# A windowed attention with a PReLU feed-forward in seven-product form: some sums kept in PSUM, bank copies that begin accumulations, 1024-column sums and splits, another ring and other combination buffers

## Chip, cores and metric

The kernel runs on one core of a Trainium2 chip. The metric is the device time of one execution in microseconds (us), lower is better; the time before is the median of three runs. Engines are named as in the profile: PE (TensorE, matmuls), PEld (its weight loads), DVE (VectorE), ACT (ScalarE), POOL (GpSimd), SP (SyncE, which here issues the DMAs). PSUM has eight banks of 512 fp32 columns by 128 partitions: PE writes its results there, and DVE and ACT read and write them.

## The reference

```python
# attention: batch 8, 8 heads, 576 positions, head size 64
scores = scale * np.matmul(q, k.transpose(0, 1, 3, 2))
mask_plain = (rel >= 0) & (rel < window)                                        # window 32, heads 0 to 3
mask_dil = (rel >= 0) & (rel < window * dilation) & (rel % dilation == 0)       # dilation 4, heads 4 to 7
scores = np.where(masks, scores, -1e9)
attn = softmax(scores)                                                          # sum + 1e-9 below
x = np.matmul(attn, v)                                                          # -> 4608 tokens x 512
# feed-forward
h = x @ w_in                                                                    # 512 x 2048
g = np.maximum(h, 0.0) + alpha * np.minimum(h, 0.0)
out = g @ w_out                                                                 # 2048 x 512
```

`w_in` and `w_out` come as 64-bit floats, all else as fp32.

## The kernel before, in words

Precision: every operand of the feed-forward is split in a high part (rounded to fp32r by an ACT copy) and a low part (the operand less its high part, a subtraction on DVE or POOL). A product is three matmuls (`PASSES`): high x high, high x low, low x high.

The tokens are nine tiles of `TT` = 512. Tiles 0 to 2 go the plain way, slice by slice of 128 hidden columns (`ffn_h`, L384, `ffn_y`, L431), while weights are loaded and converted and most pairs of heads go through attention (`Pair`). Its steps are scores (L200), maxima on DVE (L225), exponentials on ACT (L237), division on DVE (L244 to L247), transposes (L257), copies by ACT (L264), values (L275), and highs and lows or copies into the token tiles (L311 to L318). All engines' orders are written out by hand: what stands first in the code runs first on its engine.

**The combination stage.** From slice `SECOND - 1` on, POOL makes sums and differences of weight blocks for the later seven-product form (`combine`, L484 and L490, six instructions a block). Two slices later ACT rounds the result (`combined_high`, L494), DVE subtracts (`combined_low`, L498), and SP stores both parts (L502, L504). The results stand in two buffers, first in tag xB1, then in xA1. In a slice with scores, `combined_low` stands between the attention's scores and its maxima. The bank of the first scores is used next by a following `ffn_h`.

**The paired stage.** Tiles 3 to 8 go in three passes of two tiles, each pass in four groups, so twelve groups. A group takes two "units" of 256 hidden columns (j = 0, 1). Two token tiles by two halves of the model, and the same for the hidden columns, are multiplied as 2 x 2 block matrices with seven products instead of eight. A group has 28 steps of PE of six matmuls each: 14 for the hidden half (seven products q in `HORDER`, each for both j, `Four.mm`, L593) and 14 for the output half (seven products in `YORDER`, each for two column blocks m, `Out.mm`, L678). Every step takes one 256 KB weight block from a ring of `NRING` slots (`take`) and asks SP for the block that comes that many steps later (`feed`, L530).

Products of the hidden half accumulate in bank A (q 1, 6, 5, 3), B (q 2) and C (q 7, 4) of each unit. ACT saves bank A after q 1 (`s1`) and after q 6 (`s2`) and C after q 7 (`s7`), L620; DVE adds them back: 21 = C + s2, 22 = A + s7, 11 = B + s1 (L624), all into SBUF; 12 is A itself. The activation takes two instructions: `negative` on ACT (L634), `value` on DVE (L638). Then come the operands of the output half: T1 = 21 - 22, T2 = 11 - T1, T3 = 11 - 21, T4 = 12 - T2 on DVE (L645), and for each of the seven a high part on ACT (L648) and a low part (L652; "22" on DVE, the other six on POOL), all for each unit by itself, in 512 columns. The output products use 22, T1, T2, 11, T3, 12, T4 in the order of `YORDER`. After each product its bank is added to a running result in SBUF (L689; in the first group of a pass partly ACT copies, L687), 14 additions a group; in the last group of a pass the results are stored (L692).

`hidden` and `attention` put these operations at numbered steps. Attention for the last twelve pairs of heads lies in the first six groups, two pairs in each. In the last group of the first two passes the tiles of the next pass are split as well (`token_parts`, L573 to L578).

## Time and profile before

| | us |
|---|---|
| median of three runs | 1023.18 (1021.03 to 1023.5) |
| the profiled execution, own time | 1020.69 |
| its span, first to last instruction | 1018.9 |
| PE busy (share of the span) | 887.7 (87%) |
| DVE busy | 717.7 (70%) |
| ACT busy | 480.0 (47%) |
| POOL busy | 336.3 (33%) |
| mean granted clock of PE | 0.940 |

Busy time is summed per engine over the span, so it mixes stages with different limits. In a row of the timeline stand the start, the duration, engine, line, operation, output<-inputs and, in brackets, how long the engine had been idle and who released it. In a row of the lines view stand line, engine, operation, names, shapes and count, then busy us and mean ns of one, then idle time before. A row of the waits has who waited for whom, us in total, times, longest.

### The profile page before, as it was taken

The numbers are of one execution on the slowest core, as the hardware profiler recorded it, in microseconds if no ns is written. First come the engines' busy times: TensorE is split into PE (matmuls) and PEld (weight loads), VectorE is DVE, ScalarE is ACT, GpSimd is POOL, SyncE is SP. The second block draws the span as 40 slices with busy tenths as digits, with TensorE's granted clock in tenths as the row PEclk, the third lists the DMA queues.
The fourth block names the chain that finished last, engine by engine and source line by source line (L and its number), as shares of the span: only waits on it lengthen the run. The fifth ranks groups of instructions, "written<-read, shape, count | busy, mean of one in ns | idle before, by whom it ended". The sixth has DMA issues, their size and how long they took to land.

```text
span 1018.9 us, 21283 instructions
## 1 busy us (share of the span) xinstructions
PE 887.7 (87%) x7936; PEld 705.3 (69%) x7936; DVE 717.7 (70%) x1743; ACT 480.0 (47%) x1342; POOL 336.3 (33%) x250
## 2 busy tenths in 40 slices
PE   4679999898988989898989879898979797978887
PEld 4467888686877778676767657676758575766665
DVE  6997687877677666848666796848484877474756
ACT  6865555445354544554353554645242435333241
POOL 0000000407448930423324270606053527060615
PEclk9779999998999899999999989998989899989899
DMA  9730393169866664765656647664636484746452
GB/s 342 265 124 24 125 357 122 50 208 287 277 220 193 201 204 160 242 188 158 201 168 190 182 144 249 180 202 128 167 120 191 112 266 133 193 117 180 134 156 103
DMA packets 124229, 185.02 MB, mean 182 GB/s; under 512 B 9824, under 2 KB 61152, under 8 KB 124128
## 3 DMA queue, kind: packets, MB, share of 16 engines
q1 hardware_dynamic: 124128, 183.68, 58.5%
q8 instruction: 63, 1.03, 0.4%
q14 instruction: 38, 0.31, 0.1%
HBM read 143.79 MB, written 39.85 MB: 180 GB/s over the span
## 4 chain that ended last, share of the span: by engine, by line
PE 53%; DVE 27%; ACT 9%; issue 6%; POOL 3%; DMA 2%; SPq 0%; DVEq 0%; ACTq 0%; POOLq 0%
PE h L384 12%; PE y L431 10%; PE yA L678 8%; PE pA L593 7%; PE pC L593 5%; DVE stage L645 4%; DVE n L638 4%; DVE stage L638 4%; PE yB L678 3%; DVE stage L624 3%; PE yC L678 3%; ACT gp L648 2%; PE o L275 2%; ACT stage L634 2%; PE t L257 1%
## 5 line engine op out<-in xcount | busy, mean ns | idle before, releaser
L652 POOL TENSOR_TENSOR gp<-stage,gp 128x512 fp32r<-128x512 f32 x96 | 143.0, 1499 | 380.2 <-ACT gp L648 357.5
L384 PE MATMUL h<-x,w_dt.float32r 128*128 128x512 f32 x576 | 155.6, 424 | 19.6 <-DVE nm L225 19.2
L384 PEld LDWEIGHTS h<-x,w_dt.float32r 128*128 128x128 f32 x576 | 117.8, 208 | 46.7 <-issue 19.4
L431 PE MATMUL y<-g,w_dt.float32r 128*128 128x512 f32 x576 | 140.8, 393 | 0.0
L431 PEld LDWEIGHTS y<-g,w_dt.float32r 128*128 128x128 f32 x576 | 106.8, 188 | 22.7 <-ACT ob L443 0.4
L237 ACT ACTIVATE pr<-pr,nm 128x64 f32<-128x64 f32 (+1 forms) x240 | 80.5, 338 | 24.1 <-DVE nm L225 24.0
L645 DVE TENSOR_TENSOR stage<-n,stage 128x512 f32<-128x512 f32 x72 | 88.5, 1245 | 0.8
L484 POOL TENSOR_TENSOR wsum_xB<-w_dt.float32r 128x512 f32<-128x512 f32 x10 | 14.5, 1468 | 217.6 <-PE t L257 191.1
L648 ACT CAST gp<-stage 128x512 fp32r<-128x512 f32 x120 | 70.2, 613 | 26.1 <-DVE stage L645 25.8
L652 POOL TENSOR_TENSOR gp<-n,gp 128x512 fp32r<-128x512 f32 x48 | 78.1, 1626 | 0.0
L678 PE MATMUL yA<-gp,ring_w 128*128 128x512 f32 x192 | 57.4, 445 | 19.4 <-ACT gp L648 17.1
L678 PE MATMUL yA<-gp,ring_xA 128*128 128x512 f32 x192 | 56.5, 438 | 20.1 <-ACT gp L648 18.3
L411 ACT CAST g<-m 128x512 fp32r<-128x512 f32 x48 | 29.8, 621 | 80.2 <-DVE m L406 73.3
L689 DVE TENSOR_TENSOR py<-yA,py 128x512 f32<-128x512 f32 x78 | 53.0, 684 | 20.3 <-PE yA L678 20.1
L678 PE MATMUL yA<-gp,gp 128*128 128x512 f32 x144 | 46.3, 451 | 22.2 <-ACT gp L648 19.4
L624 DVE TENSOR_TENSOR stage<-pC,stage 128x512 f32<-128x512 f32 x24 | 16.5, 687 | 68.0 <-PE pC L593 64.1
L225 DVE CUSTOM_DVE_ANT_0 pr<-s,mask_sb 128x64 f32<-128x64 f32 (+1 forms) x288 | 45.1, 211 | 26.8 <-PE s L200 25.9
L678 PEld LDWEIGHTS yA<-gp,ring_w 128*128 128x128 f32 x192 | 39.5, 212 | 34.1 <-ACT gp L648 19.5
L620 ACT COPY stage<-pA 128x512 f32<-128x512 f32 x48 | 27.8, 583 | 74.8 <-PE pA L593 74.8
L678 PEld LDWEIGHTS yA<-gp,ring_xA 128*128 128x128 f32 x192 | 38.5, 207 | 34.7 <-ACT gp L648 21.3
L634 ACT ACTIVATE stage<-stage 128x512 f32<-128x512 f32 x48 | 30.1, 632 | 57.8 <-DVE stage L624 57.5
L678 PEld LDWEIGHTS yA<-gp,gp 128*128 128x128 f32 x144 | 29.4, 214 | 35.0 <-ACT gp L648 22.2
(135 smaller groups left out, 1874.0 us busy)
## 6 DMA issues: line engine op xcount, KB each, us to landing
ring_w<-wS SPq DMA_DIRECT2D x56, 256.0 KB, 2.9
ring_xA<-wS SPq DMA_DIRECT2D x56, 256.0 KB, 2.9
gp<-wS SPq DMA_DIRECT2D x56, 256.0 KB, 2.8
ring_w<-wO SPq DMA_DIRECT2D x56, 256.0 KB, 2.8
ring_xA<-wO SPq DMA_DIRECT2D x56, 256.0 KB, 2.9
gp<-wO SPq DMA_DIRECT2D x56, 256.0 KB, 3.0
v<-vW SPq DMA_DIRECT2D x24, 576.0 KB, 4.9
k<-kT SPq DMA_DIRECT2D x24, 288.0 KB, 4.4
```

What stands on the lines that cost most here:

```text
L237: nc.scalar.activation(out=self.pr[rows, r, :], in_=self.pr[rows, r, :], func=AF.Exp, bias=self.nm[rows, r:r + 1], scale=-1.0, accum_out=s ...
L384: nc.tensor.matmul(ms[t, f], lhsT=weight(0, a, f)[:, c * P:(c + 1) * P], rhs=half(t, c)[:, e, :], start=(c == 0 and n == 0), stop=(c == NC ...
L431: nc.tensor.matmul(ys[t][c], lhsT=weight(1, a, f)[:, c * P:(c + 1) * P], rhs=g[:, e, :], start=(first and n == 0), stop=(last and n == 2),)
L593: nc.tensor.matmul(to, lhsT=w[:, (2 * a + c) * P:(2 * a + c + 1) * P], rhs=part_of(name, e)[:, c * TT:(c + 1) * TT], start=start and c == ...
L624: nc.vector.tensor_tensor(out=self.x[n], in0=self.banks[bank], in1=self.x[term], op=ALU.add)
L634: nc.scalar.activation(out=self.m[n], in_=self.at(n), func=AF.Relu, scale=-1.0)
L638: nc.vector.scalar_tensor_tensor(out=self.m[n], in0=self.m[n], scalar=bal[:, f:f + 1], in1=self.at(n), op0=ALU.mult, op1=ALU.add)
L645: eng.tensor_tensor(out=self.x[n], in0=self.m[a], in1=self.x[b] if b[0] == "T" else self.m[b], op=ALU.subtract)
L648: nc.scalar.copy(out=self.g(n)[:, 0], in_=self.x[n] if n[0] == "T" else self.m[n])
L652: eng.tensor_tensor(out=g[:, 1], in0=self.x[n] if n[0] == "T" else self.m[n], in1=g[:, 0].bitcast(F32), op=ALU.subtract)
L678: nc.tensor.matmul(self.banks[what, m], lhsT=w[:, (2 * j + a) * P:(2 * j + a + 1) * P], rhs=g[:, e], start=start and j == 0 and n == 0, st ...
L689: nc.vector.tensor_tensor(out=to, in0=bank, in1=to, op=ALU.add)
```

## The change

- **Hidden half** (class `Hidden` for both units at once, in place of `Four`). Bank B is begun by an ACT copy of bank A after q 1 (`begin`), and q 2 accumulates on it, so 11 lies in B without an addition. 21 and 22 are added into PSUM (21 into its own bank C, 22 into a new bank D). `negative` and `value` read PSUM and write the wide SBUF tiles. T1, T2, T3 are one subtraction of 1024 columns for both units, and so are the high and low parts of 22, T1, 11, T2, T3, T4; T4's subtraction and the parts of 12 stay at 512. Low parts of 22, T1, T2, T3 are on DVE, those of 11, 12, T4 on POOL.
- **Output half.** Bank B is begun by an ACT copy of bank A after q 1, bank E after q 6; q 2 accumulates on B, q 3 on E, q 7 and q 4 on A. Five products are followed by an addition for each m (ten a group; plain DVE copies in the first group of a pass) into SBUF; 02, the sum of q 5, is added once to 22 and 12 at the end of a pass. `YORDER` changes from 1, 5, 6, 3, 7, 2, 4 to 1, 5, 6, 2, 7, 3, 4.
- **Attention in the groups** uses one pair of banks for scores, transposes and values, and the second pair of heads starts one step later. The split of the next tiles is placed a little later.
- **Ring**: ten slots in place of twelve; w2_1 holds the running 02 instead. Before the first group, four blocks are asked for at other slices, and six at the end.
- **Combination**: buffers also in xA0 and, later, a third one in w2_1; from the sixth block on, rounding comes three slices after POOL's work, not two. `combined_low` stands behind the maxima, the first exponentials, and the highs and lows of its slice.

```diff
-NRING = 12
+NRING = 10
...
     def combined(k):
-        tag = "xB1" if k < 5 else "xA1"
+        if k < 5:
+            tag, n = "xB1", k % 2
+        elif k < 9:
+            tag, n = ("xA1", "xA0")[(k - 5) // 2], (k - 5) % 2
+        else:
+            tag, n = (("xA1", 0), ("xA1", 1), ("w2_1", 0))[k % 3]
         if tag not in sums_at:
-            sums_at[tag] = const.tile([P, 2, 4, 2 * P], F32, tag=tag, name=f"wsum_{tag}")
-        return sums_at[tag][:, k % 2]
+            sums_at[tag] = const.tile([P, 1 if tag == "w2_1" else 2, 4, 2 * P], F32, tag=tag, name=f"wsum_{tag}")
+        return sums_at[tag][:, n]
...
-    YORDER = (1, 5, 6, 3, 7, 2, 4)
+    YORDER = (1, 5, 6, 2, 7, 3, 4)
...
-        if n >= 8:
-            return gblock(2, n // 2 - 4).rearrange("p e n -> p (e n)")[:, n % 2 * TT:(n % 2 + 1) * TT]
-        tag = ("w2_1", "w3_1", "xA1", "xA1")[n // 2]
+        if n >= 6:
+            return gblock("")[:, (n - 6) // 2, n % 2]
+        tag = ("w3_1", "xA1", "xA1")[n // 2]
...
+    def wide(n):
+        if n not in stage:
+            stage[n] = gbuf([P, GP, TT], F32, f"stage{n}", n)
+        return stage[n]
+
+    GPLACES = ("22", "12", "11", "T1", "T2", "T3", "T4", "")
...
+    def gblock(name):
+
+        n = GPLACES.index(name)
+        if n // 2 not in gts:
+            gts[n // 2] = const.tile([P, 2, 2, GP, TT], F32R, tag=f"w{n // 2}_0", name=f"gp_{n // 2}")
+        return gts[n // 2][:, n % 2]
...
+            yts[r] = const.tile([P, NC if r else 2, TT], F32, tag=f"xC{r - 1}" if r else "w2_1", name=f"py_{r}")
+        return yts[r][:, 2 * (col - 1) + m if r else m]
...
-    class Four:
...
-            self.x = {"s1": small(j, 0), "s7": small(j, 1), "s2": small(j, 2)}
-            self.x["11"], self.x["22"], self.x["21"] = self.x["s1"], self.x["s7"], self.x["s2"]
-            self.x["T2"], self.x["T1"], self.x["T4"] = self.x["s1"], self.x["s7"], self.x["s2"]
...
+    class Hidden:
...
+            self.x = {"s7": wide(0), "s2": wide(1), "21": wide(2), "22": wide(3), "11": wide(4)}
+            self.x["T1"], self.x["T2"], self.x["T3"], self.x["T4"] = wide(0), wide(1), wide(2), wide(0)
...
             what = {1: "A", 6: "A", 5: "A", 3: "A", 2: "B", 7: "C", 4: "C"}[q]
-            if q in (1, 2, 7):
-                tag = f"a{self.j}" if what == "A" else f"a{2 + self.j}"
-                self.banks[what] = psp.tile([P, TT], F32, tag=tag, name=f"p{what}_{self.id}")
-            product(self.banks[what], q, take(), q in (1, 2, 7))
+            if q in (1, 7):
+                self.bank(what, j, f"a{j}" if what == "A" else f"a{2 + j}")
+            product(self.banks[what, j], q, take(), q in (1, 7))
             feed()
...
-        def snap(self, name):
-            nc.scalar.copy(out=self.x[name], in_=self.banks["C" if name == "s7" else "A"])
-
-        def add(self, n):
-            bank, term = {"21": ("C", "s2"), "22": ("A", "s7"), "11": ("B", "s1")}[n]
-            nc.vector.tensor_tensor(out=self.x[n], in0=self.banks[bank], in1=self.x[term], op=ALU.add)
-
-        def at(self, n):
-            return self.banks["A"] if n == "12" else self.x[n]
...
+        def begin(self, j):
+            self.bank("B", j, f"y{j}")
+            nc.scalar.copy(out=self.banks["B", j], in_=self.banks["A", j])
+
+        def snap(self, name, j):
+            nc.scalar.copy(out=self.x[name][:, j], in_=self.banks["C" if name == "s7" else "A", j])
+
+        def add(self, n, j):
+            bank, term = {"21": ("C", "s2"), "22": ("A", "s7")}[n]
+            to = bank
+            if n == "22":
+                to = "D"
+                self.bank(to, j, f"a{2 + j}")
+            nc.vector.tensor_tensor(
+                out=self.banks[to, j], in0=self.banks[bank, j], in1=self.x[term][:, j], op=ALU.add)
...
+        BANK = {"11": "B", "12": "A", "21": "C", "22": "D"}
+
+        def negative(self, n, j):
+            nc.scalar.activation(out=self.of(n, j), in_=self.banks[self.BANK[n], j], func=AF.Relu, scale=-1.0)
+
+        def value(self, n, j):
+            f = 2 * self.i[j] + int(n) // 20
+            nc.vector.scalar_tensor_tensor(
+                out=self.of(n, j), in0=self.of(n, j), scalar=bal[:, f:f + 1], in1=self.banks[self.BANK[n], j],
+                op0=ALU.mult, op1=ALU.add)
...
+        def sum(self, n, eng, j=None):
+            a, b = {"T1": ("21", "22"), "T2": ("11", "T1"), "T3": ("11", "21"), "T4": ("12", "T2")}[n]
+            if j is None:
+                eng.tensor_tensor(out=self.x[n], in0=self.x[a], in1=self.x[b], op=ALU.subtract)
...
-            eng.tensor_tensor(out=self.x[n], in0=self.m[a], in1=self.x[b] if b[0] == "T" else self.m[b], op=ALU.subtract)
...
-        TO = {1: ("A", "11", 0), 5: ("C", "22", 0), 6: ("A", "12", 0), 3: ("C", "12", 2), 7: ("A", "22", 2),
-              2: ("B", "11", 2), 4: ("A", "21", 1)}
+        BANK = {1: "A", 5: "X", 6: "A", 2: "B", 7: "A", 3: "E", 4: "A"}
+        TO = {5: "02", 2: "11", 7: "22", 3: "12", 4: "21"}
...
-            what = self.TO[q][0]
-            start = q in (1, 2, 5)
+            what = self.BANK[q]
+            start = q in (1, 5)
             if start:
-                self.banks[what, m] = psp.tile(
-                    [P, TT], F32, tag=f"y{m if what == 'A' else 2 + m}", name=f"y{what}_{self.t}_{self.grp}_{m}")
-            w = take()
-            place = GPLACES.index(GBLOCKS[q])
+                self.bank(what, m, f"y{m}" if q == 1 else f"y{2 + m}")
...
-        def add(self, q, m):
-            what, n, kind = self.TO[q]
-            bank, to = self.banks[what, m], result(int(n), m)
-            if self.grp == 0 and kind < 2:
-                nc.scalar.copy(out=to, in_=bank)
+        def begin(self, what, m):
+
+            self.bank(what, m, f"a{m}" if what == "B" else f"y{2 + m}")
+            nc.scalar.copy(out=self.banks[what, m], in_=self.banks["A", m])
+
+        def after(self, q, m):
+            if q in (1, 6):
+                self.begin("B" if q == 1 else "E", m)
+                return
+            n = int(self.TO[q])
+            bank, to = self.banks[self.BANK[q], m], result(n, m)
+            if self.grp == 0:
+                nc.vector.tensor_copy(out=to, in_=bank)
             else:
                 nc.vector.tensor_tensor(out=to, in0=bank, in1=to, op=ALU.add)
-            if self.grp + 1 == NGRP and kind:
-                c, t = 2 * (int(n) // 20) + m, self.t + int(n) % 10 - 1
+            if self.grp + 1 == NGRP and q != 5:
+                if q in (7, 3):
+                    nc.vector.tensor_tensor(out=to, in0=to, in1=result(2, m), op=ALU.add)
+                c, t = 2 * (n // 20) + m, self.t + n % 10 - 1
                 nc.sync.dma_start(out=outT[c * P:(c + 1) * P, t * TT:(t + 1) * TT], in_=to)
...
-            u.tags = [[f"{side}{2 + k}" for k in range(2)], [f"{side}{k}" for k in range(2)], [f"{side}{2 + k}" for k in range(2)]]
+            u.tags = 3 * [[f"{side}{2 + k}" for k in range(2)]]
...
-            put(n, op("snap", "s1"))
-            put(n + 2, op("snap", "s7"))
-            put(n + 4, op("snap", "s2"))
-            put(n + 6, op("add", "21"), op("negative", "21"))
-            put(n + 7, op("value", "21"))
-            put(n + 8, op("add", "22"), op("negative", "22"))
-            put(n + 9, op("value", "22"), op("sum", "T1", dve))
-            put(n + 10, op("add", "11"), op("negative", "11"), op("high", "22"), op("low", "22", dve),
-                op("high", "T1"), op("low", "T1", pool))
-            put(n + 11, op("value", "11"), op("sum", "T2", dve))
-            put(n + 12, op("negative", "12"), op("high", "T2"), op("low", "T2", pool))
-            put(n + 13, op("value", "12"), op("high", "11"), op("low", "11", pool), op("sum", "T3", dve))
-            put(n + 14, op("high", "12"), op("sum", "T4", dve))
-            put(n + 15, op("high", "T3"), op("low", "T3", pool), op("low", "12", pool))
-            put(n + 16, op("high", "T4"), op("low", "T4", pool))
+            for j in range(GP):
+                put(n + j, op("begin", j))
+                put(n + 2 + j, op("snap", "s7", j))
+                put(n + 4 + j, op("snap", "s2", j))
+                put(n + 6 + j, op("add", "21", j), op("negative", "21", j))
+                put(n + 7 + j, op("value", "21", j))
+            for j in range(GP):
+                put(n + 8 + j, op("add", "22", j), op("negative", "22", j))
+                put(n + 9 + j, op("value", "22", j))
+                put(n + 10 + j, op("negative", "11", j))
+                put(n + 11 + j, op("value", "11", j))
+                put(n + 12 + j, op("negative", "12", j))
+                put(n + 13 + j, op("value", "12", j))
+            put(n + 10, op("sum", "T1", dve), op("high", "22"))
+            put(n + 11, op("low", "22", dve), op("high", "T1"))
+            put(n + 12, op("low", "T1", dve))
+            put(n + 13, op("sum", "T2", dve), op("high", "11"))
+            put(n + 14, op("high", "T2"), op("low", "11", pool))
+            put(n + 15, op("low", "T2", dve), op("high", "12", 0), op("high", "12", 1), op("low", "12", pool, 0),
+                op("low", "12", pool, 1))
+            put(n + 16, op("sum", "T3", dve))
+            put(n + 17, op("high", "T3"))
+            put(n + 18, op("low", "T3", dve))
+            put(n + 19, op("sum", "T4", dve, 0), op("sum", "T4", dve, 1))
+            put(n + 20, op("high", "T4"), op("low", "T4", pool))
 
...
-                        put(n + 14 + 2 * k + m, lambda q=q, m=m, out=out: out.add(q, m))
+                        put(n + 14 + 2 * k + m, lambda q=q, m=m, out=out: out.after(q, m))
+                hidden(n, u)
                 if t == NSTD or (todo and grp < 2):
                     attention(n + (3 if n == 0 else 1), "y", 7)
-                    attention(n + 16, "a", 7)
+                    attention(n + 17, "a", 7)
...
-        combine_at[n] = split_at[n + 2] = *todo[k], k
+        combine_at[n] = split_at[n + (2 if k < 5 else 3)] = *todo[k], k
...
-        if n in split_at:
-            combined_low(*split_at[n])
         if scored:
             scored.maxima()
             scored.exponentials(0, 5)
         if valued and valued is not pairs[2 * NC]:
             valued.highs()
             valued.lows()
+        if n in split_at:
+            combined_low(*split_at[n])
         if scored:
             scored.exponentials(5)
         for u in pairs[2 * NC:AHEAD + 1]:
@@ -1032,11 +1075,11 @@
             plan_parts()
         for op in late_ops.pop(n, ()):
             op()
-        if n >= NS - 8 and n != NS - 4:
+        if n in (NS - 7, NS - 6, NS - 2, NS - 1):
             feed()
 
     ffn_y(*slices[-1])
-    for _ in range(NRING - 7):
+    for _ in range(NRING - 4):
         feed()
```

89 lines of the change are left out of this document (38 added, 51 removed).

## The prediction

> **What bounds the kernel now.** The page comes first, for the span and for how long a weight block takes to land.
>
> ```profile
> span 1018.9 us, 21283 instructions
> ...
> ring_w<-wS SPq DMA_DIRECT2D x56, 256.0 KB, 2.9
> ```
>
> The profiled execution took 1020.69 us by its own time, 1.8 more than its span; the median of the three runs is 1023.18, 2.5 above it. All sums below are made on 1020.7, and 2.5 is added at the end.
>
> Next the windows view, cut at the group boundaries of the paired stage (columns: length; PE, PEld, DVE, ACT, POOL busy; granted clock; DMA share; GB/s).
>
> ```profile
> 503.00:556.70 53.70, 47.50 (x468) 36.87 (x467) 37.24 (x96) 24.58 (x76) 17.71 (x12) 0.97 0.62 181
> 556.70:618.90 62.20, 51.77 (x468) 39.97 (x467) 46.87 (x104) 30.66 (x82) 24.09 (x14) 0.89 0.59 179
> ...
> 824.90:870.90 46.00, 40.58 (x169) 32.23 (x169) 30.26 (x34) 20.05 (x36) 18.04 (x12) 0.96 0.66 199
> ...
> 919.00:967.10 48.10, 41.45 (x170) 32.91 (x169) 30.49 (x38) 15.88 (x28) 17.70 (x12) 0.93 0.57 154
> ...
> sum 621.90, PE 540.03 PEld 421.34 DVE 421.49 ACT 270.45 POOL 226.78; mean PE 45.00 PEld 35.11 DVE 35.12 ACT 22.54 POOL 18.90
> ```
>
> The twelve groups take 621.9 us, six tenths of the span. No engine is full in any of them, so I look for what PE waits for. First a group without attention, 919 to 967, in the timeline.
>
> ```profile
> 918.87 2.88 PE L593 MATMUL pA<-parts_w,ring_xA 128*128 128x512 f32 x12
> ...
> 928.66 0.69 DVE L624 TENSOR_TENSOR stage<-pC,stage 128x512 f32<-128x512 f32 x1 [8.90 <-PE pC L593]
> ...
> 937.27 1.28 POOL L652 TENSOR_TENSOR gp<-stage,gp 128x512 fp32r<-128x512 f32 x1 [25.28 <-ACT gp L648]
> ...
> 937.91 0.84 PE L678 MATMUL yA<-gp,ring_xA 128*128 128x512 f32 x3
> ...
> 943.04 4.51 PE L678 MATMUL yA<-gp,ring_xA 128*128 128x512 f32 x9 [4.29 <-ACT gp L648]
> ...
> 945.51 1.65 DVE L645 TENSOR_TENSOR stage<-n,stage 128x512 f32<-128x512 f32 x1
> ...
> 952.94 3.29 PE L678 MATMUL yA<-gp,gp 128*128 128x512 f32 x12 [2.35 <-ACT gp L648]
> ...
> 966.95 1.30 PE L593 MATMUL pA<-parts_w,gp 128*128 128x512 f32 x5
> ```
>
> Twelve products take 2.72 us start to start, 0.227 each, so one unit of six is 1.36 and 28 units are 38.1. The group takes 48.1: ten are lost. The hidden half loses nothing (918.87 to 937.91 is 14 units). The loss lies in the output half: PE stops after three products, waits 4.29 for the block "22" of the second unit, then runs at half clock, and waits 2.35 again for T2. The chain behind this starts at 928.66, when DVE adds the first "21", and runs through DVE and ACT for each unit in turn. POOL makes it longer: its subtraction of 512 columns takes 1.28 alone, and the DVE sum at 945.51, with both operands in SBUF, takes 1.65 beside it where the same shape from PSUM takes 0.69 (rows below). So latency bounds this stage, not throughput.
>
> With attention (503 to 556.6) it is the same picture with three more waits.
>
> ```profile
> 502.89 2.88 PE L593 MATMUL pA<-parts_w,gp 128*128 128x512 f32 x12
> ...
> 513.81 0.69 DVE L624 TENSOR_TENSOR stage<-pC,stage 128x512 f32<-128x512 f32 x1 [5.16 <-PE pC L593]
> ...
> 517.67 0.80 PE L257 MATMUL t<-ident,pr 128*128 128x128 f32 x5 [1.24 <-DVE pr L247]
> ...
> 529.90 0.49 PE L678 MATMUL yA<-gp,gp 128*128 128x512 f32 x1 [2.53 <-ACT gp L648]
> ...
> 539.80 3.29 PE L678 MATMUL yA<-gp,ring_w 128*128 128x512 f32 x12 [1.58 <-ACT gp L648]
> ```
>
> The stage ahead of the groups (223 to 397) is read in its waits and in PE's timeline.
>
> ```profile
> PE h L384 <- DVE nm L225: 14.0, 8, 3.5
> ```
>
> ```profile
> 249.87 5.44 PE L384 MATMUL h<-x,w_dt.float32r 128*128 128x512 f32 x12 [3.52 <-DVE nm L225]
> ...
> 281.87 3.00 PE L384 MATMUL h<-x,w_dt.float32r 128*128 128x512 f32 x12 [1.24 <-DVE nm L225]
> ...
> 309.02 0.98 PE L200 MATMUL s<-k,q 64*32 64x64 f32 x72
> 309.93 1.25 PE L275 MATMUL o<-pt,v 64*64 64x32 f32 x72
> 313.18 4.59 PE L384 MATMUL h<-x,w_dt.float32r 128*128 128x512 f32 x12 [2.00 <-DVE nm L225]
> ...
> 364.41 4.58 PE L384 MATMUL h<-x,w_dt.float32r 128*128 128x512 f32 x12 [1.50 <-DVE nm L225]
> ```
>
> ```profile
> 310.26 1.92 DVE L498 TENSOR_TENSOR wsum_xA<-wsum_xA,wc 128x1024 f32<-128x1024 f32 x1 [1.04 <-ACT wc L494]
> ```
>
> Each second slice, `ffn_h` needs the bank that the attention scores leave, so it waits for DVE's maxima; these stand on DVE behind `combined_low`, which itself waits 1.04 for ACT's cast and takes 1.92. After such waits the twelve h products take 4.6 to 5.4 instead of 3.0: PE has fallen to half clock.
>
> **The change, part by part.** Durations for the new instructions come from the lines view, mostly from the same operation at the same size elsewhere in this kernel.
>
> ```profile
> L689 DVE TENSOR_TENSOR py<-yA,py 128x512 f32<-128x512 f32 x78 | 53.0, 684 | 20.3 <-PE yA L678 20.1
> ...
> L574 DVE TENSOR_TENSOR parts_w<-raw_xB,parts_w 128x1024 fp32r<-128x1024 f32 x14 | 18.1, 1299 | 7.0 <-ACT parts_w L573 7.0
> ...
> L638 DVE SCALAR_TENSOR_TENSOR n<-n,bal,pA 128x512 f32<-128x512 f32 x24 | 17.6, 735 | 0.0
> ...
> L624 DVE TENSOR_TENSOR stage<-pC,stage 128x512 f32<-128x512 f32 x24 | 16.5, 687 | 68.0 <-PE pC L593 64.1 <-ACT pr L237 3.9
> ...
> L573 ACT CAST parts_w<-raw_xB 128x1024 fp32r<-128x1024 f32 x14 | 14.6, 1050 | 13.1 <-DVE raw_xB L578 12.2 <-POOL raw_xB L578 0.9
> ...
> L634 ACT ACTIVATE n<-pA 128x512 f32<-128x512 f32 x24 | 14.2, 591 | 0.0
> ...
> L393 ACT ACTIVATE h<-h 128x512 f32<-128x512 f32 x23 | 13.6, 590 | 0.0
> ...
> L578 DVE TENSOR_TENSOR raw_xB<-raw_xB 128x1024 f32<-128x1024 f32 x3 | 3.7, 1224 | 0.1
> ...
> L578 POOL TENSOR_TENSOR raw_xB<-raw_xA,raw_xB 128x1024 f32<-128x1024 f32 x1 | 2.4, 2407 | 19.2 <-DVE parts_w L574 19.2
> ```
>
> *Priced at nothing.* NRING 12 to 10: a block is issued ten units, 13.6 us, ahead, and lands in 2.9. SP's queue keeps its order of feeds; the last four of the first filling wait for the last `ffn_y`, as before, and the first is used six units, 8 us, later. Cover gone, each late block would cost up to 2.9. The attention banks on one pair instead of two: the transposes wait for maxima that were read five units earlier. The ACT copies that begin banks B and E write PSUM from PSUM, as L393 does in 0.59; four of them take the place of four DVE additions a group, two more of the two copies `s1`.
>
> *Hidden half, group without attention, on the clock of the group shown.* Add (0.69), negative (0.59), value (0.735) follow each other four times: 2.02 each, from 928.66 to 936.7. Before, the additions of "11" and the four single sums lay between. The addition into PSUM is not in this trace; below it could be 0.61 (how closely these follow each other), above 1.30 (the row of twice the width). I take 0.69, the row with the same inputs. Then DVE runs T1 (1.22) to 937.95 while ACT rounds both "22" at once (1.05) to 937.8; value 11 of the first unit to 938.7; the low part of "22" (1.30) to 940.0. PE's first product can go at 938.7, when y0 is free, and the other five of its unit at 940.0: the unit ends at 941.1 where 939.3 is undisturbed. Lost: 1.85.
>
> *Output half.* DVE goes on: value 11 to 940.7, low T1 to 942.0. ACT has rounded "11" by 941.8, so POOL takes its 1024-column subtraction (2.41) when low T1 ends and holds until 944.4. That DVE really stands behind such a POOL instruction is seen here:
>
> ```profile
> 568.88 2.69 DVE L638 SCALAR_TENSOR_TENSOR stage<-stage,bal 128x512 f32<-128x512 f32 x1 [0.70 <-ACT stage L634]
> ```
>
> (a value of 512 columns, beside POOL's 2.4 us difference). So T2, which could start at 942.7, runs 944.4 to 945.6; its high part ends at 946.7, its low part at 948.0. The T1 products end at 945.2; those of T2 can do one at 946.7 and the rest at 948.0: lost 2.6. The two "12" on POOL take turns with T3, and the last is ready 0.45 late. T3, 11 and T4 arrive at least 0.5 us before they are used. Of bank A, PE may write the second product only after ACT has copied it; the copies end by 947.3 and 952.8, and the products they hold back come at 948.0 and 953.6: nothing. New on ACT is that the first of these copies waits for DVE's value 12, whose bank it takes (942.7 and 946.3); behind it stand the roundings of T2 and "12", and their times above include that. Sum of waits 4.9, end 961.85 instead of 966.95: 5.1 gained. Four such groups: 20.4; the one that takes 46.0, 3.0.
>
> *Groups with attention.* Here 53.7 = 38.1 + two times 2.9 for scores, transposes and values + 9.8 lost. The division of the first pair is still late by 1.24. Behind it DVE's chain runs from 513.8 for 8.1, 0.5 more for the division in between, then T1 1.2, the attention's copies 0.4, a value 0.7 and the low part 1.3: "22" is ready at 526.0. PE is busy until 502.9 + 19.0 + 2.9 + 1.24 = 526.1: nothing lost there. T2 behind POOL costs 1.3 beside the scores, "12" 0.45, the second transposes about 1, and partial waits as now about 1.3: 5.3 lost, 4.5 gained, five times: 22.5. In the two groups that also make token parts (62.2 the longer) the values no longer read two SBUF tensors, so the 2.69 above becomes 0.74; with four DVE instructions of 0.68 fewer I put 6 each: 12.
>
> *Combination stage.* `combined_low` behind maxima, highs and lows: seven slices are concerned. Their waits for maxima are 14.0 less the 1.24 at 281.87, which has none in front, so 12.8; with the maxima started at the end of the scores, h follows the values (1.25) at once. Five of those h (249.87 to 364.41) run slow: 2.4 and four times 1.6, 8.8. Together 21.6. Queued behind the moved instruction now are the next `ffn_parts`, division and transposes: per pair of slices I find the division about 0.9 late, seven times 6.3. Left: 15. A third buffer and one more slice only give POOL room; the two stores behind each `combined_low` on SP move with it, and their blocks are read in later groups.
>
> *The clock.* What remains as waits may still trip it:
>
> ```profile
> 943.04:947.55 4.51, 4.51 (x10) 3.29 (x11) 4.47 (x4) 2.85 (x6) 3.91 (x3) 0.50 0.24 58
> ```
>
> ```profile
> 950.60:952.94 2.34, 0.00 (x1) 0.03 (x1) 2.34 (x4) 1.66 (x3) 2.34 (x2) 1.00 0.58 187
> ```
>
> After 4.29 idle it stood at 0.50 for about 4.5 us, after 2.34 not at all, and after 1.5 with only small products ahead it did (364.41). The T2 wait (1.5, one product, 1.3) lies between. I charge five of twelve groups with 1.6 (4.6 less 3.0): 8.
>
> Sum: 20.4 + 3.0 + 22.5 + 12 + 15 - 8 = 64.9; 1020.7 - 64.9 = 955.8; with 2.5, 958.
>
> **The rivals.** *The clock never drops in the new groups.* For: 2.34 idle left it alone. Against: 364.41. Then 958 - 8 = 950. The Trainium skill (TensorE: Matmul & The Clock Gate, "What's actually happening") says that half rate comes after at least one idle window of about 3.4 us; by that rule no wait of the new groups trips it, and the trace agrees at 4.29 and 2.34 but not at 1.50.
>
> *DVE and POOL collide more.* If one more 1024-column POOL instruction gets in front of DVE's chain in each group (the low part of "11" ahead of low T1 instead of behind it), 2.41 twelve times, 29: 987. For: in groups with attention ACT does exponentials too, and its cast of "11" and DVE's low T1 may change places. Against: low T1 starts 1.1 us before POOL could, where I worked it out. The Trainium skill (SBUF — State Buffer, "SBUF: two separate sides") says the pair of ports goes to whoever starts first, for the whole instruction; the 2.69 above agrees, and it speaks against widening anything on POOL.
>
> *The gain in the groups is used up* by waits that I don't see, and only the combination stage is left: 1023 - 15 = 1008.
>
> *Slower: the additions into PSUM.* Four stand in series at the head of the chain of every group. Each 0.1 us on them costs 12 x 0.4 = 4.8. From 0.69 + 65 / 48 = 2.04 us each the change gains nothing; at 2.4 the time is 958 + 82 = 1040. For: no row shows DVE writing PSUM. Against: ACT does it at 0.59, no slower than into SBUF (0.591).
>
> **How the numbers follow.** The forecast has 0.57, with a range of its own of 942 to 975; the clock rival 0.20, the collision 0.12, the used-up gain 0.04, the PSUM rival 0.07 (0.05 slower, 0.02 near its break-even point). Low end: no clock charge (8) and T2 not held by POOL (1.7 x 12 = 20) give 930. High end: additions at 1.30 give 958 + 29 = 987, and so does the collision; I take 988. Outside lie the last two rivals and the tails, under 2 in 10. Faster by over 0.3%, about what a measurement of this kernel can tell from none: 0.57 + 0.20 + 0.12 + 0.04 = 0.93; within it 0.02; slower 0.05.
>
> **What would show it.** Right: groups without attention of 43 to 45 us; PE's first wait in the output half under 2 us and ended by a DVE low part, not an ACT high one; T2 on DVE starting as POOL's low "11" ends; adds into PSUM near 0.7; in 223 to 397 no PE wait on maxima above 0.3 and h products at 3.0. Wrong: groups still at 46 or more; a DVE addition to PSUM above 1 us; PE held by ACT's begin copies; `ffn_parts` behind `combined_low` holding h or the transposes by more than 1 us per pair of slices.

## The result and the profile after

The changed kernel takes 964.4 us (median of four, 961.0 to 967.7) where the kernel before, on the same chip, takes 1023.3: the ratio is 0.9417, 95% interval 0.9362 to 0.9473. The prediction was 958, with 930 to 988. A second series gave 965.6 (five, ratio 0.9439, 0.9414 to 0.9463), which is used below where runs are compared. The profiled execution took 967.7 us, 53.0 less than the one before.

The page of the changed kernel:

```profile
span 965.9 us, 20972 instructions
...
PE 864.9 (90%) x7936; PEld 696.4 (72%) x7936; DVE 690.3 (71%) x1695; ACT 482.6 (50%) x1294; POOL 231.6 (24%) x154
```

PE's busy time falls by 23 us, DVE's by 27, POOL's from 336 to 232. The windows view, cut at the groups that answer to those shown of before (with attention, with attention and token parts, the 46.0 one, a plain one), and the sum of all twelve:

```profile
493.90:541.90 48.00, 44.76 (x468) 36.03 (x467) 33.21 (x89) 25.74 (x74) 10.21 (x4) 1.00 0.69 204
541.90:599.60 57.70, 48.53 (x467) 38.92 (x466) 44.70 (x101) 31.64 (x80) 14.58 (x6) 0.91 0.66 198
...
785.80:829.70 43.90, 39.49 (x170) 31.23 (x169) 33.35 (x39) 17.81 (x27) 8.33 (x4) 1.00 0.69 211
...
873.70:918.00 44.30, 40.81 (x170) 32.54 (x169) 26.60 (x31) 17.21 (x26) 8.30 (x4) 0.96 0.57 167
...
sum 570.90, PE 518.15 PEld 413.86 DVE 393.24 ACT 273.30 POOL 119.48; mean PE 43.18 PEld 34.49 DVE 32.77 ACT 22.77 POOL 9.96
```

The groups take 570.9 where they took 621.9: 51.0 less, for a forecast of 49.9. The plain group in the timeline, whose instructions can be laid beside the schedule of the prediction:

```profile
873.67 2.88 PE L600 MATMUL pA<-parts_w,ring_w 128*128 128x512 f32 x12
...
883.46 0.70 DVE L639 TENSOR_TENSOR pC<-pC,stage 128x512 f32<-128x512 f32 x1 [8.90 <-PE pC L600]
...
893.74 0.47 PE L702 MATMUL yA<-gp,ring_xA 128*128 128x512 f32 x1 [0.86 <-ACT stage L652]
...
894.83 2.79 PE L702 MATMUL yA<-gp,ring_xA 128*128 128x512 f32 x11 [0.61 <-DVE gp L677]
...
896.65 2.39 POOL L677 TENSOR_TENSOR gp<-stage,gp 128x1024 fp32r<-128x1024 f32 x1 [28.70 <-ACT gp L670]
897.14 2.98 DVE L663 TENSOR_TENSOR stage<-stage,stage 128x1024 f32<-128x1024 f32 x1
...
901.59 0.50 PE L702 MATMUL yA<-gp,gp 128*128 128x512 f32 x1 [1.25 <-ACT gp L670]
...
902.85 4.38 PE L702 MATMUL yA<-gp,gp 128*128 128x512 f32 x11 [0.76 <-DVE gp L677]
...
917.98 1.29 PE L600 MATMUL pA<-parts_w,gp 128*128 128x512 f32 x5
```

Counted from the group's start, the first output product goes at 20.1 (forecast 19.8), the other eleven at 21.2 (21.1), T2 ends on DVE at 26.4 (26.7), and the last of T2's products go at 29.2 (29.1). T2 stands behind POOL's 1024 columns as forecast: 2.98 us for what takes 1.22 alone. PE's waits are 0.86, 0.61, 1.25 and 0.76, and eleven products then take 4.38 instead of 2.79, so the half clock is there. The additions into PSUM take 0.70.

In the groups with attention the schedule of the prediction does not hold. PE's waits in the group from 493.9 and in the one from 541.9 (columns: total, times, longest):

```profile
PE t L257 <- DVE pr L247: 3.2, 2, 1.9
```

```profile
PE t L257 <- DVE pr L247: 9.2, 2, 7.0
```

There is no wait for T2 in these two: PE waits for divisions alone. Whether T2 stands behind POOL differs from group to group. In the group from 599.6, which takes 48.0, DVE starts T2 0.10 us before POOL starts the low part of "11", and it is POOL that is held; in the next one, which takes 51.0, POOL starts 0.06 us before DVE, and PE waits for T2's low part:

```profile
625.05 1.22 DVE L663 TENSOR_TENSOR stage<-stage,stage 128x1024 f32<-128x1024 f32 x1
625.15 3.38 POOL L677 TENSOR_TENSOR gp<-stage,gp 128x1024 fp32r<-128x1024 f32 x1 [40.59 <-ACT gp L670]
...
673.10 2.39 POOL L677 TENSOR_TENSOR gp<-stage,gp 128x1024 fp32r<-128x1024 f32 x1 [32.80 <-ACT gp L670]
673.16 3.41 DVE L663 TENSOR_TENSOR stage<-stage,stage 128x1024 f32<-128x1024 f32 x1
...
679.02 2.79 PE L702 MATMUL yA<-gp,gp 128*128 128x512 f32 x11 [0.76 <-DVE gp L677]
```

In the seven groups with attention or token parts T2 takes 1.22, but for this one.

The stage ahead of the groups is the disappointment. From the scores at 230 to the first paired product the windows view gives, for the kernel before and the changed one:

```profile
229.79:396.92 167.13, 151.74 (x1919) 124.01 (x1918) 117.46 (x361) 74.51 (x260) 95.79 (x84) 0.94 0.70 218
```

```profile
232.07:395.01 162.94, 149.69 (x1919) 122.17 (x1918) 118.33 (x361) 74.15 (x260) 98.42 (x84) 0.96 0.70 219
```

It is 4.2 shorter, not 15. (The scores at its start come 2.3 later than before in this profile, 0.7 in the second; the 53.0 includes that.) PE's waits in this stretch of the changed kernel:

```profile
PE o L275 <- issue: 4.0, 1, 4.0
PE t L257 <- DVE pr L247: 3.8, 4, 1.8
PE o L275 <- ACT pt L264: 2.6, 1, 2.6
PE h L384 <- DVE nm L225: 1.3, 1, 1.3
PE s L200 <- DVE m L406: 1.0, 2, 0.7
PE s L200 <- DMA q<-qT: 0.6, 1, 0.6
```

The wait for maxima fell from 14.0 to 1.3, just as forecast, but four others stand in its place. The longest is seen in PE's timeline, at the slice in which the second half of the token tile begins:

```profile
258.30 0.41 PE L257 MATMUL t<-ident,pr 128*128 128x128 f32 x2 [1.85 <-DVE pr L247]
...
270.25 0.43 PE L275 MATMUL o<-pt,v 64*64 64x32 f32 x6 [3.96 <-issue]
270.62 5.13 PE L431 MATMUL y<-g,w_dt.float32r 128*128 128x512 f32 x12
...
286.39 0.98 PE L200 MATMUL s<-k,q 64*32 64x64 f32 x72
```

PE stands still for 3.96 us ahead of the last six value products for nothing that the trace names; in the kernel before the same six waited 0.16. ACT and DVE then wait for these products (3.06 and 3.22 us), while POOL goes on. From the transposes to these products it is 12.0 us here and 5.7 there (260.63 to 266.34); with the half clock after the stop (5.13 for twelve) the stretch from one scores to the next, 262.9 to 286.4, is 9 us longer than before.

### The profile page after: what moved, and what is told of

Same layout as the page of the kernel before. It is cut to its first block, busy times and chain, and to the rows that moved or that the text cites. A ratio compares the mean times of both kernels' runs of the same rounds, so it can differ in the third digit from the quotient of the medians.

```text
span 965.9 us, 20972 instructions
## 1 busy us (share of the span) xinstructions
PE 864.9 (90%) x7936; PEld 696.4 (72%) x7936; DVE 690.3 (71%) x1695; ACT 482.6 (50%) x1294; POOL 231.6 (24%) x154
## 3 DMA queue, kind: packets, MB, share of 16 engines
q8 instruction: 63, 1.03, 0.4%
## 4 chain that ended last, share of the span: by engine, by line
PE 48%; DVE 34%; ACT 7%; issue 5%; DMA 3%; POOL 1%; SPq 1%; DVEq 0%; ACTq 0%; POOLq 0%
PE h L384 10%; PE y L431 9%; PE yA L702 8%; PE pA L600 7%; DVE gp L677 5%; DVE stage L663 4%; PE pC L600 4%; DVE stage L656 3%; PE o L275 3%; PE yE L702 2%; ACT stage L652 2%; DVE py L721 2%; PE yB L702 2%; PE s L200 2%; DVE pD L639 2%
## 5 line engine op out<-in xcount | busy, mean ns | idle before, releaser
L677 POOL TENSOR_TENSOR gp<-stage,gp 128x1024 fp32r<-128x1024 f32 x24 | 62.2, 2590 | 415.4 <-ACT gp L670 377.6
L670 ACT CAST gp<-stage 128x1024 fp32r<-128x1024 f32 x72 | 75.5, 1049 | 62.2 <-DVE stage L663 46.7
L677 DVE TENSOR_TENSOR gp<-stage,gp 128x1024 fp32r<-128x1024 f32 x48 | 64.2, 1336 | 10.8 <-ACT gp L670 10.8
L225 DVE CUSTOM_DVE_ANT_0 pr<-s,mask_sb 128x64 f32<-128x64 f32 (+1 forms) x288 | 45.4, 212 | 26.4 <-PE s L200 25.7
L639 DVE TENSOR_TENSOR pC<-pC,stage 128x512 f32<-128x512 f32 x24 | 16.7, 696 | 65.0 <-PE pC L600 61.5
L663 DVE TENSOR_TENSOR stage<-stage,stage 128x1024 f32<-128x1024 f32 x36 | 61.1, 1697 | 1.0
L702 PEld LDWEIGHTS yA<-gp,ring_xA 128*128 128x128 f32 x240 | 44.3, 188 | 20.2 <-DVE gp L677 3.9
L600 PE MATMUL pA<-parts_w,ring_xA 128*128 128x512 f32 x228 | 56.8, 397 | 0.9 <-DMA ring_xA<-wS 0.9
L600 PE MATMUL pA<-parts_w,gp 128*128 128x512 f32 x228 | 55.8, 392 | 1.2 <-ACT pB L628 1.2
L679 POOL TENSOR_TENSOR gp<-n,gp 128x512 fp32r<-128x512 f32 x24 | 47.8, 2010 | 20.8 <-ACT gp L672 20.5
L600 PEld LDWEIGHTS pA<-parts_w,ring_xA 128*128 128x128 f32 x228 | 43.2, 191 | 10.1 <-issue 1.1
L600 PEld LDWEIGHTS pA<-parts_w,gp 128*128 128x128 f32 x228 | 42.5, 188 | 10.7 <-ACT pB L628 1.6
```

The costliest lines, as they stand in the source:

```text
L225: nc.vector.tensor_tensor_reduce(out=self.pr[rows, r, :], in0=self.ps[e][rows, g, :], in1=mask_sb[rows, kind, :], scale=-SCALE, scalar=3.0 ...
L600: nc.tensor.matmul(to, lhsT=w[:, (2 * a + c) * P:(2 * a + c + 1) * P], rhs=part_of(name, e)[:, c * TT:(c + 1) * TT], start=start and c == ...
L639: nc.vector.tensor_tensor(out=self.banks[to, j], in0=self.banks[bank, j], in1=self.x[term][:, j], op=ALU.add)
L663: eng.tensor_tensor(out=self.x[n], in0=self.x[a], in1=self.x[b], op=ALU.subtract)
L670: nc.scalar.copy(out=g[:, 0], in_=self.x[n])
L677: eng.tensor_tensor(out=g[:, 1], in0=self.x[n], in1=g[:, 0].bitcast(F32), op=ALU.subtract)
```

## The experiments

Each kernel below is one edit of the changed kernel unless it says otherwise, and was timed against the kernel before. Lengths of the stage and of groups come from one profile of each kernel.

### Where the stage's gain went

**The changed kernel again**, unaltered.

> The changed kernel, unaltered, for its spread and a second profile. In the first profile the paired stage began at 395.0 us where the kernel before had 396.9, though each pair of slices with scores ran in 13.8 us instead of 17. Some 9 us were lost between 262.9 and 286.4, with a stop of 3.96 us ahead of the last six value products in which no engine had work. Theory 'chance': the stop is not of the change; a second profile without it has the paired stage begin near 386 to 389 us and a time of 958 to 962. Rival 'lateness': the moved split pushes its wait to this place, the stop is there again, the stage begins near 395 and the time is 964 to 968.

965.6 us. The stop is there again, 3.68, and the stage from the scores on takes 162.7 (393.14 less 230.48). It is no chance: each of the ten profiles with the moved split shows a stop of 1.75 to 4.2 at these six products, and none of the four with the old order more than 0.2.

**The order undone.** `combined_low` again ahead of `scored.maxima()`:

```
+        if n in split_at:
+            combined_low(*split_at[n])
         if scored:
             scored.maxima()
...
-        if n in split_at:
-            combined_low(*split_at[n])
```

> The changed kernel with one thing undone: the low part of a combined block stands ahead of the attention maxima on DVE again, as before the change. Theory 'order' (the forecast's own term: seven waits for maxima and five h at half clock are gone by the order alone): 11 to 15 us slower, 975 to 979, with PE waits on maxima of 1.5 to 3 us in front of the h products again. Rival 'lateness': the order gains nothing that is not given back in the same stage, 963 to 967.

969.0 (0.9471, 0.9452 to 0.9491): 3.4 slower, far from 11 to 15. PE's waits in the stage:

```profile
PE h L384 <- DVE nm L225: 13.1, 8, 3.3
```

The waits for maxima are back, the six products run on without a stop, and the stage takes 166.9.

**Groups alone, stage alone.** The first has the whole combination stage of before (`combined` with two buffers, `split_at[n + 2]`, the order above) and the new groups. The second is the kernel before with `combined`, `split_at[n + (2 if k < 5 else 3)]` and the order of the change; its ring keeps twelve slots, but eight of the first twelve blocks are asked for only at the end, as `w2_1` now holds a buffer.

> The changed kernel with the whole combination stage of before (two buffers, split two slices later, low part ahead of the maxima); only the paired groups are changed. Theory 'order': the groups are worth 50 to 51 us, the time is 1023 less 50, 972 to 974, and the paired stage begins near 397. Rival 'lateness': the combination was worth 2, so 966 here.

> The kernel before with the combination stage of the change alone (combined buffers, split three slices later for the last eleven blocks, low part behind maxima, highs and lows); the ring keeps its twelve blocks, the first four fed in the last four slices and eight behind them. Theory 'order': 1023 less 11 to 15, 1008 to 1012, paired stage begins 382 to 386. Rival 'lateness': 1019 to 1023.

967.4 (0.9462, 0.9441 to 0.9484) and 1021.2 (0.9976, 0.9957 to 0.9995). So the groups are worth 55.6 by the medians (51.7 by their length in the profiles, 622.0 and 570.3; the profiled execution of before lies 2.3 under the median of this series), and the stage about 2. Both speak for 'lateness' as to size.

**The stores moved**, to see whether the transfers eat the gain:

```
+    LATER = (16, 17, 18, 19, 20, 21, 23, 24)
...
-        elif 0 <= n - SECOND < CUT:
-            save(n - SECOND + CUT)
+        elif n in LATER:
+            save(CUT + LATER.index(n))
```

> The changed kernel with the plain weight stores of the last eight 128-column blocks moved from slices 24 to 31 to slices 16 to 24, where the DMA share is low; arithmetic and order of the engines unaltered. In both profiles of the changed kernel all engines stop for 3.7 to 4.0 us ahead of the last six value products near 266 us, waiting for nothing that the trace names, while the DMA share is 104 to 112% from 262 to 267.5 us and an instruction transfer lands late in it; the kernel before has the same instruction with 0.16. Theory 'queue': the moved split puts its stores in one bunch with the plain stores, the attention loads and the instruction transfer, and that bunch eats what the order gained. Then the stop falls below 0.7, scores wait for no load, the paired stage begins 6 to 9 us earlier (385 to 388) and the time is 957 to 960. Rival 'code': the stop belongs to the place in the program and stays near 3.7; the time stays 963 to 967. Rival 'lateness': the divisions behind the split hold the stage in any case; the stop goes, the time gains under 2.

962.6 (0.9394, 0.9362 to 0.9426). The interval overlaps that of the changed kernel; the profile is clearer, with the stage and the stop:

```profile
228.94:386.69 157.75, 146.94 (x1919) 120.25 (x1919) 118.31 (x361) 74.00 (x260) 98.82 (x84) 0.98 0.62 193
```

```profile
263.65 0.31 PE L275 MATMUL o<-pt,v 64*64 64x32 f32 x6 [1.85 <-issue]
```

The stage is 157.8, 5 less than 162.7 and 162.9: the stop is halved, and the products after it are less slow (4.40 for 5.13). The paired stage begins at 386.7, as 'queue' expected; the time lies above its 957 to 960. Rival 'code' is right as to the place, which is the same six products in every profile with a stop, and not as to the size. What keeps the time up: half of the stop stays, and in this profile a second group with attention has T2 behind POOL (3.21) and takes 51.0 instead of 48.0.

**Stores moved and order undone:**

> The stores moved as in the run above and the low part of a combined block ahead of the maxima again. Theory 'queue': the order is worth its forecast (11 to 15) once the DMA is out of the way, so this is 968 to 973 where the run above is 957 to 960, as slow as the order undone with the stores in place (969.0). Rival 'lateness': the two lie within 4 us of each other.

969.3 (0.9451, 0.9424 to 0.9478). Its stage:

```profile
229.22:395.33 166.11, 151.12 (x1919) 123.29 (x1918) 120.52 (x361) 74.23 (x260) 95.66 (x84) 0.95 0.58 183
```

166.1, no shorter than 166.9 with the stores in place. So the order is worth 8.4 us in the stage when the stores are out of the way (166.1 less 157.8; 6.7 by the medians) and 4.2 when they are not (3.4 by the medians). 'Queue' was right in kind; it makes 4 to 5 of the missing 11 by these profiles and about 3 by the medians. The kernels further down show how far single profiles scatter: with the stores moved the stage takes 160.0 and 159.4, with the stores in place 162.6, 162.8, 161.0 and 160.4. Nor does the length of the stop tell the loss by itself. In the kernel with "11" on DVE below, whose stores are in place, the six products stop for only 1.75, the scores ahead of them wait 2.01 for `ffn_parts` where they waited 0.66, and the stage takes 162.6 all the same.

What the stop is: in the transfers' view of the second profile of the changed kernel, the share of the 16 engines' time is 106 to 112% from 262 to 267, and an instruction transfer of 16 KB lands at 266 to 267; PE goes on at 268.8. With the stores moved it lands at 261 to 262 and PE goes on at 263.7; in the kernel before at 263 to 264, and the six products come at 266.3. With "11" on DVE and the stores in place it lands at 265 to 266 and PE goes on at 267.6. PE's restart follows that transfer by 1.6 to 3.3 in each. The Trainium skill (Runtime: NRT & Kernel Launch, "Instruction fetch mechanics") says that an engine's instructions are fetched in blocks of 16 KiB by a DMA queue of its own, at a cost that is mostly hidden; the 63 instruction transfers of 1.03 MB agree in size, and here a cost was seen at the time of one. If they are PE's, its 15872 matmuls and weight loads make 252 for each transfer. That PE waited for its instructions is argued from these coincidences and not shown; no run took the transfer away.

### What sets the groups

**The lock on T2.** The low part of "11" moves from POOL to DVE, behind the low part of T3:

```
-            put(n + 14, op("high", "T2"), op("low", "11", pool))
+            put(n + 14, op("high", "T2"))
...
-            put(n + 18, op("low", "T3", dve))
+            put(n + 18, op("low", "T3", dve), op("low", "11", dve))
```

> The changed kernel with the low part of block '11' taken from POOL (1024 columns, 2.4 us, ahead of T2) and put on DVE behind the low part of T3; it is used six units after that. Theory 'lock': T2 on DVE (2.98 us beside POOL, 1.22 alone) starts and ends 1.7 us earlier in each group, PE's waits for T2 fall from 1.27 and 0.77 to under 0.6 and the half clock after them (4.38 for eleven products instead of 2.78) goes: 1.6 and 1.6 less in a plain group, 1.5 in one with attention, in all 24 to 34 us: 931 to 941. Rival 'throughput': POOL's help is needed, the 1.22 more on DVE in each group comes back as later T3 and T4: 960 to 968. Rival 'port is no lock': T2's 2.98 has another cause and stays, 965 or a little more.

953.3 (0.9298, 0.927 to 0.9326). The plain group that took 44.3:

```profile
864.48 2.88 PE L600 MATMUL pA<-parts_w,ring_w 128*128 128x512 f32 x12
...
887.94 1.22 DVE L663 TENSOR_TENSOR stage<-stage,stage 128x1024 f32<-128x1024 f32 x1
...
891.88 2.79 PE L702 MATMUL yA<-gp,gp 128*128 128x512 f32 x11 [0.53 <-DVE gp L677]
...
905.44 0.84 PE L600 MATMUL pA<-parts_w,gp 128*128 128x512 f32 x3
```

41.0 from start to start: T2 takes 1.22, a wait of 0.53 is left of its two, and the eleven products take 2.79. In this group 'lock' is right to the tenth (3.2 expected, 3.3 seen); the five groups without attention gain 1.7, 2.4, 3.0, 3.3 and 1.3, together 11.7. With attention little changes: 48.2 for 48.0, and 49.9 for 51.0. In the groups of 48.0 there was no lock on T2 to take away: it takes 1.22 there in the changed kernel too. That is why the whole gain is 12 and not 24, and why the time lies outside every range. 'Port is no lock' is out, since T2 takes 1.22 in all groups now.

**A begin copy undone.** The first partial sum is kept in SBUF and added into bank B by DVE:

```
-            self.bank("B", j, f"y{j}")
-            nc.scalar.copy(out=self.banks["B", j], in_=self.banks["A", j])
+            nc.scalar.copy(out=self.x["11"][:, j], in_=self.banks["A", j])
...
-                put(n + 10 + j, op("negative", "11", j))
+                put(n + 10 + j, op("add", "11", j), op("negative", "11", j))
```

> The changed kernel with one of its copies undone: bank B of the hidden half starts empty, the first partial sum is kept in SBUF by ACT, and DVE adds it into the bank (two additions of 0.69 more per group, ahead of the negatives of '11'). Theory of the forecast (the chain of DVE ahead of the output half sets the group): both additions lie on the chain to the low part of '22' and to T2, 1.4 a group, 14 to 17 in all, 979 to 983. Rival 'T2 is set by POOL': the additions hide in the time that T2 stands behind POOL, only the first output product is later (0.7 a group): 970 to 974. Rival 'off the path': no change, 963 to 967.

965.5 (0.9416, 0.939 to 0.9442): no change that can be told. But it is not off the path, as the same plain group shows:

```profile
875.35 2.88 PE L600 MATMUL pA<-parts_w,ring_w 128*128 128x512 f32 x12
...
895.23 0.69 DVE L638 TENSOR_TENSOR pB<-pB,stage 128x512 f32<-128x512 f32 x1
...
897.10 2.77 PE L701 MATMUL yA<-gp,ring_xA 128*128 128x512 f32 x11 [1.22 <-DVE gp L676]
...
899.42 1.22 DVE L662 TENSOR_TENSOR stage<-stage,stage 128x1024 f32<-128x1024 f32 x1
...
899.60 3.30 POOL L676 TENSOR_TENSOR gp<-stage,gp 128x1024 fp32r<-128x1024 f32 x1 [28.46 <-DVE n L655]
...
904.03 2.79 PE L701 MATMUL yA<-gp,gp 128*128 128x512 f32 x11 [1.21 <-DVE gp L676]
...
917.57 1.75 PE L600 MATMUL pA<-parts_w,gp 128*128 128x512 f32 x7
```

The additions do delay the first output products (wait 1.22 for 0.61). They also delay value "11", and POOL, which waits for it, now starts after T2: T2 takes 1.22, no half clock follows, and the group is 42.2 instead of 44.3. In two groups with attention the same delay costs 2.3 each (50.3 for 48.0), while the one of 51.0, in which T2 now comes first too, takes 48.9. The price of 0.69 in the chain was about right (T2 starts 0.6 later), and a change of who comes first between DVE and POOL paid for it.

**Halves.** Each 1024-column sum, rounding and low part as two instructions of 512, in the same place (the sum is shown; the other two are changed alike):

```
             if j is None:
-                eng.tensor_tensor(out=self.x[n], in0=self.x[a], in1=self.x[b], op=ALU.subtract)
+                for j in range(GP):
+                    self.sum(n, eng, j)
...
```

> The changed kernel with every 1024-column sum, rounding and low part of the paired groups issued as two instructions of 512 columns in the same place of the order (no arithmetic changes). Theory 'fewer instructions': each width costs DVE 0.14 and ACT 0.13 more (2 x 0.68 for 1.22; 2 x 0.59 for 1.05), about 1.0 and 0.8 in a group; of this 0.3 to 0.6 lies ahead of the first output product and of T2: 3 to 8 slower, 968 to 973. Rival 'pieces': PE needs the first unit's half only, which is ready 0.6 earlier, and DVE gets in between POOL's halves, so that T2 is held 1.3 instead of 1.7: 955 to 962.

960.5 (0.9375, 0.9341 to 0.941), so 'pieces':

```profile
868.74 2.88 PE L600 MATMUL pA<-parts_w,ring_w 128*128 128x512 f32 x12
...
888.67 3.47 PE L705 MATMUL yA<-gp,ring_xA 128*128 128x512 f32 x12 [0.73 <-ACT gp L674]
...
892.22 2.83 DVE L666 TENSOR_TENSOR stage<-stage,stage 128x512 f32<-128x512 f32 x2
...
910.23 1.98 PE L600 MATMUL pA<-parts_w,gp 128*128 128x512 f32 x8
```

The first output product has no second wait after 0.73, since PE needs only the first unit's half, though its two units take 3.47 and not 2.88. T2 is still held (2.83 for 1.36). The plain group takes 41.5. In the groups with attention it costs: 49.1 for 48.1 and 50.7 for 48.0. In the changed kernel the width is no gain in itself.

**Transposes later.** The transposes, copies and values of an attention pair one unit later, the divisions where they were:

```
-            put(n + step - 1, u.divisions)
+            put(n + 6, u.divisions)
...
-                    attention(n + 17, "a", 7)
+                    attention(n + 17, "a", 8)
```

> The changed kernel with the transposes, copies and values of each attention pair in the paired groups one unit (1.36 us) later; the divisions stay where they are. In the changed kernel's groups with attention PE waits for nothing but divisions, 1.3 at the first pair and 1.9 to 2.2 at the second, and 9.2 in the group with token parts. Theory 'divisions set these groups': each wait falls by up to one unit, 1.3 and 1.36, so 2.6 in each of six groups and their slow products with it, 14 to 18 in all: 947 to 952. Rival 'the wait moves': the values or the next products are late instead (copies of the transposed part, banks a2 and a3, T2), the groups stay at 47 to 48 and the time is 961 to 967.

955.4 (0.933, 0.9295 to 0.9364), between the two. In a group that took 48.1 and now takes 47.9 PE waits for:

```profile
PE t L257 <- DVE pr L247: 0.9, 1, 0.9
PE o L275 <- ACT pt L264: 0.8, 1, 0.8
PE yA L702 <- DVE gp L677: 0.8, 1, 0.8
```

The wait for divisions fell from 3.3 to 0.9, but the copies behind the transposes and a low part took its place, and the group is no shorter: 'the wait moves', there. The low part is T2's: POOL now starts ahead of DVE in all five groups with attention and no token parts, and T2 takes 3.2 to 3.4. The 7.5 us that the twelve groups gained are in three groups that had taken 50.5, 51.0 and 44.3 and now take 48.0, 47.9 and 42.4. The last of them has no attention: in it the half clock did not come, which the edit does not explain.

**Three edits together** ("11" on DVE, stores early, transposes later), and the same with halves:

> Three edits together: the low part of '11' on DVE, the plain stores of the last eight blocks earlier, the transposes one unit later. Theory 'three places': the gains add up, since they lie in the plain groups (12), in the stage ahead (3 to 5) and in the groups with attention (14 to 18): 930 to 936. Rival 'DVE is full': with '11' on DVE the later transposes collide with T3 and T4, the sum falls short by 6 or more: 940 to 950.

> The three edits together, and every 1024-column operation of the paired groups again as two of 512. In the changed kernel the halves gained 5 us (960.5): the plain groups without final additions went from 44.0 to 41.5, since the first output product ran through (wait 0.73 instead of 0.86 and 0.61) and the half clock behind T2 was gone, while the groups with attention took 1 to 2.7 more. Theory 'same gain twice': what the halves gained in plain groups is mostly the half clock, which the low part of '11' on DVE has already removed; left are 0.6 to 0.7 in each of six, 4, against 1 or more in each of six groups with attention: 938 to 945. Rival 'pieces are better': the gains add, 931 to 935.

938.7 (0.9163, 0.9126 to 0.92) and 937.7 (0.915, 0.9122 to 0.9179). Each edit alone gave 12.3, 3.0 and 10.2; together they give 26.9 (by the ratios 14, 5 and 11, together 28). So they add up to within the noise, and 930 to 936 was missed mainly because the transposes gave less than the 14 to 18 expected. Two of the edits help each other: with "11" on DVE T2 takes 1.22 again in the groups with attention, and these fall from the 47.9 of the transposes alone to 46.8 to 47.0. The kernel is 2.8% under the changed one. The version with halves cannot be told from it: plain groups of 39.9 for 40.7, groups with attention of 47.0 to 47.7 for 46.8 to 47.0, so 'same gain twice', 0.3 under its range.

## Why the prediction was right or wrong, step by step

- *Plain groups.* Right in mechanism, the places of waits to 0.3 us. The waits are smaller than the 4.9 forecast: 1.5 at the first output product (1.85), 2.0 at T2 (2.6), none at "12" (0.45). Forecast 20.4 and 3.0 before the charge for the clock; measured, with the half clock in it, 17.5 and 2.1 (48.1, 48.1, 48.1 and 51.9 became 42.4, 44.0, 44.3 and 47.9; 46.1 became 43.9).
- *Groups with attention.* Right in size, only in part in reason. 22.5 were forecast and 21.6 came. Of the 5.3 that the step left lost, the first division (1.24) and the second transposes (about 1) came, as 1.3 and 1.9 to 2.2 in most groups. T2 behind POOL (1.3), "12" (0.45) and partial waits (1.3) did not, but for the one group of 51.0. That T2 is free in the others was in part luck and not the schedule: in three of them DVE and POOL start within 0.1 us of each other. With "11" off POOL the groups of 48.0 changed by 0.2 and the one of 51.0 by 1.1.
- *Groups with token parts.* 12 forecast, 9.8 measured: the values fell as priced, but in the first of them PE waits 9.2 for divisions, 5.6 before, since DVE has token parts ahead of them.
- *Combination stage.* The step that failed: 15 forecast, 4.2 measured. Of its terms the waits for maxima were right (12.8 forecast, 12.7 gone) and five slow h products did end (8.8), but two other steps of twelve products are slow, by 4.3. What was mis-sized is what is given back: 6.3 of later divisions were charged, and 10.5 of new waits came: 3.8 divisions, 3.8 of the stop, 1.3 copies, 1.0 the bank that `ffn_parts` still reads, 0.6 a load. About 2.5 more are not assigned. The step took account of DVE's queue and named SP's stores only as moved; that they meet the attention loads and the plain stores behind them was not priced, and moving the plain stores away brought 3 to 5 of the missing 11 back. The rest of it stays open.
- *The clock.* Rival at 0.20: it drops no more. It fell: in the first profile of the changed kernel the mean granted clock is 0.91 to 0.97 in seven of the twelve groups and 1.00 in the others, where the prediction charged five. One of the seven in the second profile, the plain group shown above, from the end of T1's products on:

```profile
898.28:899.55 1.27, 0.00 (x0) 0.00 (x0) 0.48 (x2) 1.09 (x2) 0.00 (x0) 1.00 0.76 200
899.55:900.81 1.26, 0.49 (x1) 0.19 (x1) 1.26 (x2) 1.26 (x3) 0.15 (x1) 1.00 0.50 190
900.81:905.20 4.39, 4.39 (x12) 3.48 (x13) 3.88 (x4) 1.77 (x3) 3.36 (x2) 0.61 0.18 64
```

After waits of 1.27 and 0.77, with one product between, the clock is 0.61 for 4.4 us. By the rule that the prediction quotes from the Trainium skill (TensorE: Matmul & The Clock Gate, "What's actually happening"), half rate after an idle window of about 3.4 us, it would have stayed up; this trace does not agree.
- *DVE and POOL collide more, additions into PSUM slow, gain used up.* None came: low T1 was ahead of POOL in the plain groups, additions take 0.70, and the groups kept their gain.
- *Priced at nothing.* The first group's late block cost 0.6 to 0.9 (a wait for the ring in each profile with a part of the change, also in the stage alone, whose ring has twelve slots), and one begin copy holds PE for 1.2 in the first group of the last pair of token tiles. The rest cost nothing.

The total was near because the groups' 51.0 came and the stage was a quarter of the sum; its own failed step is 11 of the 65. In the groups each part fell short of what was forecast before the charge for the clock, by 6.9 together, and 8 were charged.

## What to carry to other kernels

Before a wait is counted as gained, list every DMA and every instruction that stands behind the moved one on all queues, and look at the transfers' share in the slices into which they fall. An engine-by-engine chain holds where PE has nothing else to do (the plain groups, to a few tenths) and not where it has (attention beside it). When an edit changes who reaches a shared resource first, its price is not that of its instructions: two additions more cost nothing, and two halves for one gained 5 in one kernel and nothing that can be told in another. Where two engines come to a shared resource within a tenth of a us, forecast both outcomes: here they are 48 and 51 us for the same group.
